# A gated convolution and attention kernel: the loads as streams of their own on SyncE's queue, without GpSimd's fills, the filter's first half early, in a new order

## The chip, the cores and the metric

The kernel runs on one core of one Trainium2 chip. The metric is the device time of one execution in microseconds (us), the median of several runs. The core has five engines with queues of their own: TensorE (PE, matmuls and their weight loads, PEld), VectorE (DVE), ScalarE (ACT), GpSimd (POOL) and SyncE (SP), which here only issues DMAs. Matmuls write to PSUM; DVE and ACT copy ("evict") the results to SBUF.

## The reference

Sequence S = 2048, width D = 640, bfloat16 inputs. Two branches share the input x = A_q, and a gate mixes them.

```
k_shift = sum over t of k_pad[:, t:t+S] * shift_k[:, 3-t]        # four taps along the sequence
kv      = k_shift * v
y       = irfft(rfft(kv, 2S) * rfft(ssm_k, 2S))[:S] + kv * ssm_D # long convolution, per channel
a       = x * y

q, k, v = split(x @ wqkv) in 32 heads of 20
logits  = q . k at offsets 0, 2, ..., 14 back in the sequence, scaled, masked
b       = (softmax(logits) @ v) @ wo

g       = sigmoid(sum(x * gate_w))
out     = g * a + (1 - g) * b
```

## The kernel before

**Attention.** x is loaded in 8 tiles `xn` and transposed by PE into `xT` (`xpose`). `vproj` makes the values `VW` in two halves (weights `Wv0`, `Wv1`, both in `WvT`). `qkproj` makes q and k in five feature groups `ft` of 128 columns: for each `ft`, six units of five matmuls each for q (w = 0) and for k (w = 1). `ft` 0 uses the weights `W0` (spread by `spread` into `Wqk`), the others `W1`, the rest of `Wqk`. Units are evicted into one staging tile `stg` for q and one for k, by DVE (L247) or ACT (L245); GpSimd copies the rows of each head from `stg` into `qb` and `kb` by DMAs (`fragger`, L637: 70 in all). A staging tile is written again only when the copies of the group before it have landed. `score_gen` then makes the scores of eight groups of four heads, t = 0 to 7 (L659), ACT takes their exponentials into `ETall` (L667), `pv_gen` multiplies them with `VW` (L691), and DVE divides into `VW`'s place (L701, L703). Scores of t need the copies of every piece of its heads: t = 1 some of `ft` 1, t = 4 some of `ft` 3, t = 6 some of `ft` 4.

**Convolution.** The four taps run on DVE over `kin`, a part of the tile `KX` (L474 to L489, 56 instructions of 128x1280), then kv = k_shift * v in `vin` (L493). The filter and kv go through a transform in two matmul stages: `s1_unit` (L722 for the filter, L718 for kv) and `s2_unit` with the constants `G` (L741). The filter goes in two halves P = 0 and 1, loaded into the same tile `h_lin`; half 0 is evicted into the tile `H`, half 1 into `SX`, which takes the place of `KX` when the taps are done. kv is evicted into `UC`. Products (L773), a first inverse stage (L852), the attention's output projection (L886) and the last stage with the final sum (`final`, L929 to L946) follow. `Dz` (ssm_D) is added to the filter by one DVE instruction for each half (L790) ahead of its first stage. The gate is one group of matmuls (L541) with one activation on ACT (L545).

**Order.** Every piece of work is a generator that yields requests for engines. A string `ORDER`, one letter for each grant, says which generator goes on next and so sets the order of instructions on every engine; nothing is reordered on the chip, and an engine waits where the next instruction in its queue isn't ready. The costs and landing times in the requests do not reach the chip; they were for the making of the string.

**Loads.** `heads` issues on SyncE, ahead of all: x, `Wv0`, `W0`, then the tap weights `wraw`, the first k rows, `W1` and `Wv1`. All other loads belong to `bulk(ft)`, which `fragger` calls after each feature group: after `ft` 0 the rest of k, its corners, `F`, `wgz`, `Dz` and the filter's first half, after `ft` 1 `G` and half of v, after `ft` 2 the rest of v, after `ft` 3 the filter's second half. Most go through `paced`: GpSimd first writes one element of the destination, and the DMA on SyncE's queue waits for that fill. Each load on SyncE's queue also waits until the eighth before it has landed.

Of the kernel before, what the change touches and what calls it, by code (L numbers as in the profile page):

```python
# [17 lines left out]
S = 2048  # L18
# [109 lines left out]


# [88 lines left out]
def kernel(  # L218
# [105 lines left out]
    st = {}  # L324

    def load(name, dst, src, us, deps=()):
        g = yield Req("S", 600.0, deps, move=us)
        nc.sync.dma_start(dst, src)  # L328
        mark(name, g, 1500.0 if name[0] == "k" else 0.0)
# [6 lines left out]
    def load_k(k):  # L336
        n0, n1 = KROWS[k]
        for q in range(4):
            yield from paced(f"k{k}{q}", kin[32 * q:32 * q + 32, 3 + n0:3 + n1, :], raw(k2, n0 * D + QC * q, [[64 * D, 32], [D, n1 - n0], [1, QC]]), 62.0 * (n1 - n0))

    def load_corners():
        for q in range(4):
            for a, b in ((1, 17), (17, 32)):
                yield from load(f"kh{q}{a}", kin[32 * q + a:32 * q + b, 0:3, :], raw(k2, (64 * a - 3) * D + QC * q, [[64 * D, b - a], [D, 3], [1, QC]]), 90.0)

    def load_h(P):
        if P:
            yield Req("N", 0.0, [ev("hs10")])
        for q in range(4):
            for c in range(2):  # L350
                yield from paced(f"h{P}{q}{c}", h_lin[32 * q:32 * q + 32, :, c, :],
                                 raw(A_ssm_k, (160 * q + 80 * c + PL * P) * S, [[64, 32], [S, PL], [1, 64]]), 1280.0)

    def load_G(a):
        yield from paced(f"G{a}", G[:, 8 * a:8 * a + 8], raw(cf["G"].ap(), 3 * a * 128 * 512, [[512, 128], [128 * 512, 3], [1, 512]]), 1300.0)

    def load_v(c, q):
        yield from paced(f"v{q}{c}", vin[32 * q:32 * q + 32, c], raw(v2, QC * q + 80 * c, [[64 * D, 32], [D, 64], [1, 80]]), 2550.0)

    def small():  # L360
        g = yield Req("G", 1200.0)
        nc.gpsimd.memset(wgz[:], 0.0)
        nc.gpsimd.memset(Dz[:], 0.0)
        yield from load("F", F[:], cf["F"].ap(), 640.0, [g.done])
        yield from load("wgz", wgz[:, :, 0], gate_w.rearrange("(t p) -> p t", p=128), 200.0)
        yield from load("Dz", raw(Dz, 0, [[32 * Dz[:].ap[0][0], 4], [1, 160]]), raw(A_ssm_D, 0, [[160, 4], [1, 160]]), 100.0)

    def bulk(ft):
        if ft == 0:
            yield from load_k(1)  # L370
            yield from load_k(2)
            yield from load_corners()
            yield from small()
            yield from load_h(0)
        if ft == 1:
            for a in range(4):
                yield from load_G(a)
                yield from load_v(0, a)
        if ft == 2:
            for a in range(4):  # L380
                yield from load_v(1, a)
        if ft == 3:
            yield from load_h(1)
# [19 lines left out]
    def heads():  # L403
        z = pab[:, 0].rearrange("p n c -> p (n c)")
        nc.vector.memset(z, 0.0)
        wu = PS[:, 0]
        for n in range(WARM):
            nc.tensor.matmul(wu[:, n % 2, :], lhsT=z[:, 0:128], rhs=z[:, 0:512], start=True, stop=True, skip_group_check=True)
        nc.scalar.dma_start(ident[:], ca["ident"].ap())
        nc.scalar.dma_start(mm[:], ca["mm"].ap())  # L410
        at("ET", 4000.0)
        for a in range(8):
            if a == 1:
                nc.sync.dma_start(Wv[:, :, 0:320], W3[:, :, 2, 0:320])
# [7 lines left out]
        n0, n1 = KROWS[0]  # L422
        for q in range(4):
            nc.sync.dma_start(wraw[32 * q:32 * q + 32].rearrange("p c j -> p (c j)"), raw(A_shift_k, 4 * QC * q, [[0, 32], [1, 4 * QC]]))
        for q in range(4):
            nc.sync.dma_start(kin[32 * q:32 * q + 32, 3 + n0:3 + n1, :], raw(k2, n0 * D + QC * q, [[64 * D, 32], [D, n1 - n0], [1, QC]]))
        for q in range(4):
            at(f"k0{q}", LAND["k"][0])
        for w in range(2):
            nc.sync.dma_start(Wqk[:, :, w, 128:D], W3[:, :, w, 128:D])  # L430
            at(f"W1{w}", LAND["W1"])
        nc.sync.dma_start(Wv[:, :, 320:640], W3[:, :, 2, 320:640])
        at("Wv1", LAND["Wv1"])
# [134 lines left out]
    def qkproj():  # L568
        free = [None] * NSTG
        def unit(ft, w, k):  # L570
# [6 lines left out]
            for i in range(2):  # L577
# [10 lines left out]
                if not ft:  # L588
# [1 line left out]
                    nc.vector.scalar_tensor_tensor((ksets if w else qsets)[0][:, cols].rearrange("p (b k) -> p b k", k=wd), src, own,  # L590
                                                   mm[:, BK * (1 - w):BK * (1 - w) + wd].unsqueeze(1).to_broadcast([128, 3, wd]), ALU.mult, ALU.add)
# [30 lines left out]
    def fragger():  # L622
# [4 lines left out]
        for ft in range(NDT):  # L627
            for w in range(2):
# [359 lines left out]
```

## Time and profile before

| | us |
|---|---|
| runs: median (lowest) of 3 | 225.23 (225.09; one of 483.92) |
| profiled execution: its time | 226.57 |
| profiled execution: span from first to last instruction | 224.6 |
| busy: PE, DVE, ACT, POOL | 206.6, 190.3, 174.8, 49.8 |
| mean granted TensorE clock | 0.972 |

The page gives for each engine the busy time in the span; the views of the trace give single instructions (start, duration, engine, line, output and input tiles), who waited for whom, and busy times in chosen stretches. SPq and POOLq are the instructions with which SyncE and GpSimd issue DMAs; "to landing" is the time from such an issue until the data has arrived.

### The profile page before, as it was taken

To read this page: it belongs to the slowest core of one execution; us is meant where nothing else is said; L and a number is where in the kernel's file an instruction comes from. 1 tells how busy PE (TensorE), PEld (TensorE's weight loads), DVE (VectorE), ACT (ScalarE), POOL (GpSimd) and SP (SyncE) were. 2 spreads that over 40 slices of the span, in tenths; PEclk is the share of its full clock that TensorE was granted. 3 is DMA by queue.
4 is the path that set the end of the run, shared out by engine and by line. 5 is a ranking of instruction groups with operands and counts; after the bars stand their busy time and mean duration, and the time that the engine had idled before them with its cause. 6 is when DMAs were issued, how large, how long until landed. Compare 5 with 4: busy or idle time off the path is not lost.

```text
span 224.6 us, 8413 instructions
## 1 busy us (share of the span) xinstructions
PE 206.6 (92%) x3577; PEld 167.4 (75%) x3577; DVE 190.3 (85%) x277; ACT 174.8 (78%) x253; POOL 49.8 (22%) x132
## 2 busy tenths in 40 slices
PE   7999899999999999999996888999999999988880
PEld 3776677796768658666784767888988999977870
DVE  4787996999988988998888765899999999848991
ACT  2146672559999997899999898999899987767770
POOL 7900673180526047104520000000000000000000
PEclk9999999999999999999999758999999999999997
DMA  7999359889999999976834288777660390001755
GB/s 206 348 238 304 54 97 217 134 150 144 208 172 196 152 163 166 162 107 107 158 85 117 61 175 181 174 203 183 144 191 0 81 236 16 3 3 35 176 140 127
DMA packets 68916, 32.67 MB, mean 145 GB/s; under 512 B 51504, under 2 KB 66736, under 8 KB 68880
## 3 DMA queue, kind: packets, MB, share of 16 engines
q1 hardware_dynamic: 65488, 27.14, 59.5%
q0 software_dynamic: 2944, 4.74, 10.4%
q8 instruction: 28, 0.46, 1.0%
q10 hardware_dynamic: 448, 0.26, 0.5%
q14 instruction: 8, 0.07, 0.1%
HBM read 19.52 MB, written 2.62 MB: 99 GB/s over the span
## 4 chain that ended last, share of the span: by engine, by line
PE 62%; DMA 9%; DVE 8%; ACT 8%; SPq 4%; issue 4%; POOL 2%; ACTq 0%; DVEq 0%; POOLq 0%
PE PS L583 13%; PE PS L886 9%; PE PS L852 8%; PE PS L741 7%; PE PS L691 7%; PE PS L528 6%; DMA xn<-in_A_q_dram 5%; PE PS L659 4%; DMA WvT<-in_B_wqkv_dram 3%; SPq L328 3%; ACT ETall L667 2%; PE PS L722 2%; ACT H L245 2%; PE PS L870 2%; DVE SX L247 2%
## 5 line engine op out<-in xcount | busy, mean ns | idle before, releaser
L667 ACT ACTIVATE ETall<-PS 121x912 bf16<-121x912 f32 (+1 forms) x80 | 64.8, 868 | 7.5 <-PE PS L659 6.7
L583 PE MATMUL PS<-xT,Wqk 128*128 128x342 bf16 (+1 forms) x300 | 50.7, 310 | 0.4 <-ACT xT L245 0.2
L245 ACT CAST UC<-PS 128x1024 bf16<-128x1024 f32 (+2 forms) x48 | 43.9, 1010 | 5.4 <-PE PS L852 3.4
L583 PEld LDWEIGHTS <-Wqk 128*128 128x128 bf16 x300 | 27.9, 97 | 14.0 <-issue 0.6
L528 PE MATMUL PS<-WvT,xT 128*121 128x320 bf16 x180 | 29.6, 302 | 0.6 <-ACT ETall L667 0.5
L637 POOL DMA_DIRECT2D qb<-stg x35 | 17.7, 507 | 52.3 <-ACT stg L245 39.1
L245 ACT CAST stg<-PS 128x363 bf16<-128x363 f32 (+1 forms) x34 | 15.8, 467 | 12.7 <-DVE kb L590 4.6
L474 DVE TENSOR_TENSOR KX<-KX 128x1280 bf16<-128x1280 bf16 x32 | 25.3, 819 | 0.3
L528 PEld LDWEIGHTS <-xT 128*121 128x121 bf16 x180 | 22.8, 134 | 2.6 <-issue 0.4
L886 PE MATMUL PS<-wo,oT 128*128 128x320 bf16 x160 | 24.1, 302 | 0.0
L886 PEld LDWEIGHTS <-oT 128*128 128x128 bf16 x160 | 21.1, 146 | 1.1
L741 PEld LDWEIGHTS <-G 64*128 64x128 bf16 x512 | 19.0, 97 | 3.8 <-issue 1.9
L691 PEld LDWEIGHTS <-ETall 121*128 121x128 bf16 x576 | 18.4, 99 | 2.2 <-issue 0.9
L637 POOL DMA_DIRECT2D kb<-stg x35 | 17.4, 503 | 10.1 <-ACT ETall L667 4.0
L691 PE MATMUL PS<-VW,ETall 121*128 121x63 bf16 (+2 forms) x576 | 19.0, 188 | 0.6 <-ACT ETall L667 0.6
L247 DVE CAST UC<-PS 128x1024 bf16<-128x1024 f32 x14 | 16.7, 1219 | 3.4 <-PE PS L852 3.0
L659 PE MATMUL PS<-qb,kb 31*128 31x114 bf16 x576 | 16.3, 218 | 2.9 <-ACT ETall L667 1.0
L659 PEld LDWEIGHTS <-kb 31*128 31x128 bf16 x576 | 9.6, 96 | 11.6 <-issue 10.5
L852 PE MATMUL PS<-F,Hw 128*128 128x128 bf16 x160 | 18.1, 219 | 0.0
L852 PEld LDWEIGHTS <-Hw 128*128 128x128 bf16 x160 | 17.9, 114 | 0.1
L247 DVE CAST stg<-PS 128x342 bf16<-128x342 f32 (+1 forms) x26 | 13.5, 519 | 2.9 <-PE PS L583 2.0
L703 DVE TENSOR_TENSOR VW<-PS,rd 114x960 bf16<-114x960 f32 (+1 forms) x16 | 14.5, 907 | 0.6
(79 smaller groups left out, 340.3 us busy)
## 6 DMA issues: line engine op xcount, KB each, us to landing
xn<-in_A_q_dram SPq DMA_DIRECT2D x8, 320.0 KB, 6.2
h_lin<-in_A_ssm_k_dram SPq DMA_DIRECT2D x16, 160.0 KB, 4.5
vin<-in_A_v_dram SPq DMA_DIRECT2D x8, 320.0 KB, 11.4
Hw<-H SPq DMA_DIRECT2D x8, 320.0 KB, 3.7
q<-in_A_q_dram SPq DMA_DIRECT2D x8, 320.0 KB, 6.7
Hw<-SX SPq DMA_DIRECT2D x8, 320.0 KB, 4.6
out_dram<-q SPq DMA_DIRECT2D x16, 120.0 KB, 2.2
kb<-stg POOLq DMA_DIRECT2D x22, 85.1 KB, 5.1
```

The source lines that it names most:

```text
L245: nc.scalar.copy(dst, src)
L247: nc.vector.tensor_copy(dst, src)
L474: eng.tensor_tensor(d, kin[:, n + 3 - j:n + 3 - j + m, :], w.to_broadcast([128, m, QC]), ALU.mult)
L528: nc.tensor.matmul(ps[0:BK, 0:320], lhsT=xT[:, dt, s0:s0 + BK], rhs=Wv[:, dt, 320 * hp:320 * hp + 320], start=(dt == 0), stop=(dt == NDT - 1))
L583: nc.tensor.matmul(ps[:, 0:n], lhsT=Wqk[:, dt, w, 128 * ft:128 * ft + 128], rhs=xT[:, dt, s0:s0 + n], start=(dt == 0), stop=(dt == NDT - 1))
L637: nc.gpsimd.dma_start((ksets if w else qsets)[t % 3][r0:r0 + rows, 0:wd], stg[s0:s0 + rows, 0:wd])
L659: nc.tensor.matmul(psum(g, h4 // 2)[:, h4 % 2, BQ * bb:BQ * bb + BQ], lhsT=kb[r:r + DH + NF, BK * b:BK * b + 128], rhs=qb[r:r + DH + NF, B ...
L667: nc.scalar.activation(ETall[0:BK, e, :, 0:BQ * nb], psum(g, k)[0:BK, :, 0:BQ * nb], ACT.Exp, scale=SCALE)
L691: nc.tensor.matmul(O[:, (b - b0) // 6, c0:c0 + 21 * nh], lhsT=ETall[0:BK, e, hh, BQ * bb:BQ * bb + 128], rhs=VW[0:BK, b, 4 * t + h4:4 * t ...
L741: nc.tensor.matmul(ps[:, c, 160 * jj:160 * jj + 160], lhsT=G[rows, j0 + jj, 64 - 64 * rr:192 - 64 * rr], rhs=Am[rows, rr].rearrange("p o ( ...
L852: nc.tensor.matmul(d, lhsT=st[(key, P)][:, c, o + il // 4, :, il % 4], rhs=M[:, k, :], start=(k == 0), stop=(k == 1), skip_group_check=True)
L886: nc.tensor.matmul(op, lhsT=oT[:, ft].rearrange("p h m a -> p a (h m)")[:, t, :], rhs=wo[:, ft, 320 * n:320 * n + 320], start=(ft == 0), s ...
```

## The change

`paced` and its fills on GpSimd are gone, and so is `bulk`. The loads become generators of their own, each granted in `ORDER` by its own letter: `load_W` (W1, Wv1), `load_k` (tap weights, all k rows, corners), `load_h(P)`, `load_G` (F, Dz, G) and `load_v` (wgz, v). Their order on SyncE's queue is that of the new string. The zero fills of `Dz` and `wgz` move to the head of GpSimd's program. DVE's staging cast of `ft` 0 now names the eviction before it (`r.done`) as its dependence.

```
-    def paced(name, dst, src, us):
-        g = yield Req("G", 150.0)
-        nc.gpsimd.memset(dst[:, 0, 0:1], 0.0)
-        yield from load(name, dst, src, us, [g.done])
+    def load_W():
+        for w in range(2):
+            yield from load(f"W1{w}", Wqk[:, :, w, 128:D], W3[:, :, w, 128:D], 2000.0)
+        yield from load("Wv1", Wv[:, :, 320:640], W3[:, :, 2, 320:640], 1250.0)
...
+    def load_k():
         for q in range(4):
+            yield from load(f"wr{q}", wraw[32 * q:32 * q + 32].rearrange("p c j -> p (c j)"), ...
+        for k, (n0, n1) in enumerate(KROWS):
+            for q in range(4):
+                yield from load(f"k{k}{q}", kin[32 * q:32 * q + 32, 3 + n0:3 + n1, :], ...
...
     def load_h(P):
         if P:
             yield Req("N", 0.0, [ev("hs10")])
         for q in range(4):
             for c in range(2):
-                yield from paced(f"h{P}{q}{c}", h_lin[32 * q:32 * q + 32, :, c, :],
+                yield from load(f"h{P}{q}{c}", h_lin[32 * q:32 * q + 32, :, c, :],
...
-    def bulk(ft):
-        if ft == 0:
-            yield from load_k(1)
-            yield from load_k(2)
-            yield from load_corners()
-            yield from small()
-            yield from load_h(0)
-        if ft == 1:
-            for a in range(4):
-                yield from load_G(a)
-                yield from load_v(0, a)
...
-            yield from bulk(ft)
...
-                r = yield Req("AD", n=m, deps=[g.done] + ([free[sb]] if free[sb] is not None else []), give=g.banks)
+                r = yield Req("AD", n=m, deps=[r.done if not ft else g.done] + ([free[sb]] if free[sb] is not None else []), give=g.banks)
...
 ORDER = """
-a-aa-aw6-ww-wa-awa6-aiaiiw-6-6aiai-i-aa-aiiaiiiiii-iiiaiiiiidiwidi-wiiiiififiiwfcwcidcwficcicwccdfddfccfccfcfwicxd-iwwfcxxfdic-xcc
+a-aa3-a-333a-yy-a3a33zav-yaiii3-yi-aiz3uavi-3zaiaz-a3ii3aii3i3iii33i3-3vaiii3i-i-3iiiiiii33iv-ivcdcidi3ciccc-3iid3d3zfdwi3czzwid-3
...
```

SyncE's queue behind the x tiles (`xn`), before: tap weights (in_A_shift_k), first k rows, the W1 halves (`Wqk`), Wv1 (`WvT`), and then the loads that wait for fills.

```order
L424 DMA KX<-in_A_shift_k_dram 32x640 x4
L426 DMA KX<-in_A_k_dram 32x22x160 x4
L430 DMA Wqk<-in_B_wqkv_dram 128x5x512 x2
L432 DMA WvT<-in_B_wqkv_dram 128x5x320
L328 DMA KX<-in_A_k_dram 32x22x160 x4
L328 DMA KX<-in_A_k_dram 32x20x160 x4
```

The same place now, up to Wv1; nothing here waits for a fill.

```order
L328 DMA h_lin<-in_A_ssm_k_dram 32x40x64 x2
L328 DMA KX<-in_A_shift_k_dram 32x640 x2
L328 DMA KX<-in_A_k_dram 32x22x160
L328 DMA h_lin<-in_A_ssm_k_dram 32x40x64
L328 DMA F<-cf_F 128x512
L328 DMA h_lin<-in_A_ssm_k_dram 32x40x64 x2
L328 DMA Dz<-in_A_ssm_D_dram 4x160
L328 DMA h_lin<-in_A_ssm_k_dram 32x40x64
L328 DMA KX<-in_A_k_dram 32x22x160 x3
L328 DMA Wqk<-in_B_wqkv_dram 128x5x512
L328 DMA KX<-in_A_k_dram 32x22x160
L328 DMA WvT<-in_B_wqkv_dram 128x5x320
```

The eight loads of the filter's first half, which before stood behind all of k, now stand ahead of most of k, of the second half of W1 and of Wv1 (two filter loads, the first W1 half and two tap weights stand above these rows). The second half of the filter stands between the loads of v and G, and waits for the first half's last matmul (L693 now, L722 before).

DVE where `ft` 1's first q unit is staged (`stg`, 128x342), before; the taps (TENSOR_TENSOR on `KX`) have begun ahead of it.

```order
L497 COPY KX<-KX 128x640
L474 TENSOR_TENSOR KX<-KX 128x1280
L590 SCALAR_TENSOR_TENSOR kb_80<-PS,mm 128x363
L474 TENSOR_TENSOR KX<-KX 128x1280 x2
L590 SCALAR_TENSOR_TENSOR kb_80<-PS,mm 128x363
L483 TENSOR_TENSOR KX<-KX 128x1280
L474 TENSOR_TENSOR KX<-KX 128x1280
L487 TENSOR_TENSOR KX<-KX 128x1280
L489 TENSOR_TENSOR KX<-KX 128x1280
L474 TENSOR_TENSOR KX<-KX 128x1280
L247 CAST stg<-PS 128x342
```

The same place now.

```order
L562 SCALAR_TENSOR_TENSOR kb_80<-PS,mm 128x363
L469 COPY KX<-KX 128x640
L247 CAST VW<-PS 121x16x20
L247 CAST stg<-PS 128x342
L247 CAST VW<-PS 121x16x20
L761 TENSOR_TENSOR h_lin<-h_lin,Dz 128x80
L247 CAST stg<-PS 128x342 x2
L247 CAST VW<-PS 121x16x20
L247 CAST stg<-PS 128x342
L446 TENSOR_TENSOR KX<-KX 128x1280 x3
```

The taps have moved behind the four staging casts, and the sum of Dz to the filter's first half stands between them.

ACT ahead of the exponentials of t = 4 (`ETall`, the last row), before. The k units of `ft` 3 (`stg`, 128x363) were staged further up, the last five of them by DVE.

```order
L667 ACTIVATE ETall<-PS 121x2x342 x2
L245 CAST VW<-PS 121x16x20 x2
L245 CAST H_302<-PS 128x2x512 x2
L245 CAST stg<-PS 128x342
L245 CAST VW<-PS 121x16x20
L245 CAST stg<-PS 128x342
L245 CAST H_302<-PS 128x2x512
L245 CAST VW<-PS 121x16x20
L245 CAST H_302<-PS 128x2x512
L667 ACTIVATE ETall<-PS 121x2x456 x6
```

The same place now.

```order
L245 CAST stg<-PS 128x363
L638 ACTIVATE ETall<-PS 121x2x342
L245 CAST stg<-PS 128x363
L245 CAST VW<-PS 121x16x20
L638 ACTIVATE ETall<-PS 121x2x342
L245 CAST VW<-PS 121x16x20
L245 CAST H_336<-PS 128x80x12 x2
L638 ACTIVATE ETall<-PS 121x2x456 x2
```

The k units of `ft` 3 are now staged just ahead of t = 4; the evictions of `H` here are those of the second stage (128x80x12) and no longer those of the first (128x2x512). Behind the gate's activation and ahead of the first eviction of `UC`, ACT had 34 exponentials, 7 evictions of `H`, 10 of `SX` and 4 staging casts; it now has 24, 2, 9 and none.

More of the change, by code (lines that the diff above doesn't have):

```diff
@@ L326, in load @@
     def load(name, dst, src, us, deps=()):
-        g = yield Req("S", 600.0, deps, move=us)
+        g = yield Req("S", 450.0, deps, move=us)
         nc.sync.dma_start(dst, src)
-        mark(name, g, 1500.0 if name[0] == "k" else 0.0)
-    def paced(name, dst, src, us):
-        g = yield Req("G", 150.0)
-        nc.gpsimd.memset(dst[:, 0, 0:1], 0.0)
-        yield from load(name, dst, src, us, [g.done])
-    def load_k(k):
-        n0, n1 = KROWS[k]
+        mark(name, g)
+    def load_W():
[3 more added lines that the diff above has]
+    def load_k():
         for q in range(4):
-            yield from paced(f"k{k}{q}", kin[32 * q:32 * q + 32, 3 + n0:3 + n1, :], raw(k2, n0 * D + QC * q, [[64 * D, 32], [D, n1 - n0], [1, QC]]), 62.0 * (n1 - n0))
-    def load_corners():
+            yield from load(f"wr{q}", wraw[32 * q:32 * q + 32].rearrange("p c j -> p (c j)"), raw(A_shift_k, 4 * QC * q, [[0, 32], [1, 4 * QC]]), 200.0)
+        for k, (n0, n1) in enumerate(KROWS):
+            for q in range(4):
+                yield from load(f"k{k}{q}", kin[32 * q:32 * q + 32, 3 + n0:3 + n1, :], raw(k2, n0 * D + QC * q, [[64 * D, 32], [D, n1 - n0], [1, QC]]), 62.0 * (n1 - n0))
         for q in range(4):
             for a, b in ((1, 17), (17, 32)):
-                yield from load(f"kh{q}{a}", kin[32 * q + a:32 * q + b, 0:3, :], raw(k2, (64 * a - 3) * D + QC * q, [[64 * D, b - a], [D, 3], [1, QC]]), 90.0)
+                yield from load(f"kh{q}{a}", kin[32 * q + a:32 * q + b, 0:3, :], raw(k2, (64 * a - 3) * D + QC * q, [[64 * D, b - a], [D, 3], [1, QC]]), 150.0)
     def load_h(P):
@@ L350, in load_h @@
             for c in range(2):
-                yield from paced(f"h{P}{q}{c}", h_lin[32 * q:32 * q + 32, :, c, :],
[L352 to L365, printed above, removed]
-        yield from load("Dz", raw(Dz, 0, [[32 * Dz[:].ap[0][0], 4], [1, 160]]), raw(A_ssm_D, 0, [[160, 4], [1, 160]]), 100.0)
-    def bulk(ft):
-        if ft == 0:
-            yield from load_k(1)
-            yield from load_k(2)
-            yield from load_corners()
-            yield from small()
-            yield from load_h(0)
-        if ft == 1:
-            for a in range(4):
-                yield from load_G(a)
-                yield from load_v(0, a)
[L379 to L383, printed above, removed]
+                yield from load(f"h{P}{q}{c}", h_lin[32 * q:32 * q + 32, :, c, :],
+                                raw(A_ssm_k, (160 * q + 80 * c + PL * P) * S, [[64, 32], [S, PL], [1, 64]]), 1050.0)
@@ new lines, in load_G, with load_v @@
+    def load_G():
+        yield from load("F", F[:], cf["F"].ap(), 640.0)
+        yield from load("Dz", raw(Dz, 0, [[32 * Dz[:].ap[0][0], 4], [1, 160]]), raw(A_ssm_D, 0, [[160, 4], [1, 160]]), 100.0)
+        for a in range(4):
+            yield from load(f"G{a}", G[:, 8 * a:8 * a + 8], raw(cf["G"].ap(), 3 * a * 128 * 512, [[512, 128], [128 * 512, 3], [1, 512]]), 1500.0,
+                            [ev("Wp00"), ev("Wp01")])
+    def load_v():
+        yield from load("wgz", wgz[:, :, 0], gate_w.rearrange("(t p) -> p t", p=128), 500.0)
+        for c in range(2):
+            for q in range(4):
+                yield from load(f"v{q}{c}", vin[32 * q:32 * q + 32, c], raw(v2, QC * q + 80 * c, [[64 * D, 32], [D, 64], [1, 80]]), 2800.0)
@@ L421, in heads @@
             at(f"x{a}", LAND["x"][a])
[L422 to L433, printed above, removed]
+        nc.gpsimd.memset(Dz[:], 0.0)
+        nc.gpsimd.memset(wgz[:], 0.0)
         nc.gpsimd.memset(xT[:, :, 0:X0], 0.0)
@@ L495, in conv @@
     def conv():
-        yield Req("D", 570.0, [ev("k00")])
+        yield Req("D", 570.0, [ev("k00")] + [ev(f"wr{q}") for q in range(4)])
         nc.vector.tensor_copy(wl, wraw.rearrange("p c j -> p j c"))
@@ L535, in gate @@
     def gate():
-        g = yield Req("P", 0.0, [ev("vproj0"), ev("vproj1")] + xdeps(0, HS), take=1, pe=(20, 50.0, 110.0, 53.0))
+        g = yield Req("P", 0.0, [ev("vproj0"), ev("vproj1"), ev("wgz")] + xdeps(0, HS), take=1, pe=(20, 50.0, 110.0, 53.0))
         gps = psum(g)[:, 0]
@@ L787, in h_slot @@
         for P in range(2):
-            g = yield Req("D", 150.0, [ev(f"h{P}{q}{c}") for q in range(4) for c in range(2)])
+            g = yield Req("D", 150.0, [ev(f"h{P}{q}{c}") for q in range(4) for c in range(2)] + [ev("Dz")])
             h_ = h_lin[:, :, :, 0]
@@ L802, in h_stream @@
     def h_stream(P):
-        yield Req("N", 0.0, [ev(f"Dz{P}"), ev("SX" if P else "H0")])
+        yield Req("N", 0.0, [ev(f"Dz{P}"), ev("F"), ev("SX" if P else "H0")])
         yield from transform("h", P)
@@ L950 @@
     for gen in (xpose, h0_slot, fragger, score_gen, pv_gen, conv, conv_v, conv_end, qkproj, gate, x_slot, h_slot, p2_slot,
-                u_slot, swaps, load_T, load_wo, op_tr, outproj, final):
+                u_slot, swaps, load_T, load_wo, op_tr, outproj, final, load_W, load_k, load_G, load_v, spread):
         plan.add(gen(), gen.__name__)
-    for gen in (load_q, vproj, h_stream, u_stream, products, inverse1):
+    for gen in (load_h, load_q, vproj, h_stream, u_stream, products, inverse1):
         for P in range(2):
             plan.add(gen(P), f"{gen.__name__}{P}")
-    plan.add(spread(), "spread")
     plan.run(ORDER)
```

16 lines of the change are left out of this document (8 added, 8 removed).

## The prediction

> **What bounds the kernel now.** I read the page's first part, then the busy times by stage, then the waits and the groups inside the one stage that stands out.
>
> ```profile
> span 224.6 us, 8413 instructions
> PE 206.6 (92%) x3577; PEld 167.4 (75%) x3577; DVE 190.3 (85%) x277; ACT 174.8 (78%) x253; POOL 49.8 (22%) x132
> ```
>
> TensorE (PE) is busy for 92% of the span, and VectorE (DVE) and ScalarE (ACT) are not far below. An average of 92% can hide a stage with another limit, so the stages come next. I cut them at the first attention product, the gate, the end of the projections, the first matmul of the value transform (L718) and the last tiles. The columns are length, then busy time and count of PE, weight loads, DVE, ACT and POOL, then granted clock, DMA share and GB/s.
>
> ```profile
> 0.00:48.30 48.30, 45.23 (x393) 33.81 (x394) 38.93 (x64) 23.28 (x43) 24.25 (x61) 1.00 0.87 194
> 48.30:98.75 50.45, 50.26 (x853) 36.55 (x854) 45.98 (x70) 44.86 (x70) 17.30 (x52) 1.00 1.08 170
> 98.75:109.70 10.95, 10.79 (x212) 7.04 (x213) 9.94 (x14) 10.65 (x17) 3.50 (x7) 1.00 0.64 114
> 109.70:143.56 33.86, 28.20 (x701) 23.62 (x700) 25.56 (x32) 31.22 (x40) 4.03 (x10) 0.85 0.58 126
> 143.56:155.00 11.44, 11.16 (x107) 10.06 (x106) 11.11 (x11) 11.44 (x14) 0.19 (x1) 1.00 0.89 222
> 155.00:199.40 44.40, 44.37 (x738) 41.88 (x735) 40.95 (x69) 38.71 (x51) 0.54 (x2) 1.00 0.38 89
> 199.40:219.50 20.10, 16.61 (x587) 14.48 (x587) 16.99 (x22) 14.64 (x22) 0.00 (x0) 1.00 0.40 99
> ```
>
> Three things are to be seen. Up to 109.7 us PE hardly stops after the first loads, while ACT is busy only 23.28 of the first 48.30 us. From 109.70 to 143.56 us PE loses 5.66 us and its clock falls to 0.85, while ACT is busy 92%: this stage belongs to ACT. From 155 to 199.4 us PE is the limit again. The change fills ACT's idle front with the filter's first half; its gain, if any, must show in the fourth row.
>
> **The loads.** SyncE's queue before, and the price of GpSimd's staging copies with quiet and with loaded DMA engines:
>
> ```profile
> 16.89 1.06 SPq L432 DMA_DIRECT2D WvT<-in_B_wqkv_dram  x1
> 30.68 14.10 SPq L328 DMA_DIRECT2D KX<-in_A_k_dram  x16
> 47.00 9.87 SPq L328 DMA_DIRECT2D h_lin<-in_A_ssm_k_dram  x8
> 24.14 3.12 POOL L637 DMA_DIRECT2D qb<-stg  x6 [12.37 <-ACT stg L245]
> 20.00:30.00 10.00, 8.92 (x85) 6.64 (x86) 8.73 (x15) 7.08 (x15) 5.56 (x11) 1.00 0.51 127
> qb<-stg POOLq DMA_DIRECT2D x2, 32.1 KB, 2.9
> qb<-stg POOLq DMA_DIRECT2D x5, 80.2 KB, 6.3
> kb<-stg POOLq DMA_DIRECT2D x1, 68.1 KB, 5.3
> 6.64 6.90 DMA xn<-in_A_q_dram
> ```
>
> The queue lies idle from 17.95 to 30.68 us, because the fills stand behind twelve copies on GpSimd; DMA runs at half share there. The fills themselves (0.1 us each, on an engine busy 22%) are worth nothing on the path. Without them the queue goes on at once. Will the weights be late, now that the filter stands ahead of them? The last x tile lands at 13.5 us (6.64 + 6.90). Ahead of the second half of Wqk stand eight filter loads (9.87 us by the row above), four k loads (4/16 of 14.10 is 3.5 us), the first Wqk and small ones (some 3 us): landing near 32 us with its own transfer. PE reaches the first matmul that reads it only after 39.6 us of its own work in the new order (summed at the prices of the next part), so nothing waits, with about 8 us of cover; if the cover were gone, DVE's convolution would also stand behind the k loads, microsecond for microsecond.
>
> **ACT's backlog behind the gate.** The work that PE has moved to in front of the gate's matmuls is, by the two orders, 35 projection matmuls, 72 scores, 72 attention products and 96 second-stage filter matmuls. Their prices:
>
> ```profile
> 71.00 0.72 PE PS L583 x5
> 51.92 0.32 PE PS L659 x16
> 109.69 1.45 PE PS L691 x48
> 142.27 1.36 PE PS L741 x36
> 99.99 0.60 ACT L545 ACTIVATE WvT<-PS 128x512 f32<-128x512 f32 x1 [0.22 <-PE PS L541]
> 145.30 1.01 ACT L245 CAST UC<-PS 128x1024 bf16<-128x1024 f32 x1
> ```
>
> That is 7 x 0.72 + 4.5 x 0.32 + 1.5 x 1.45 + 2.67 x 1.36 = 12.3 us, so ACT's gate activation, which ended at 100.59, ends near 112.9. What ACT then still has to do before the first eviction of the value transform, priced from these groups:
>
> ```profile
> L667 ACT ACTIVATE ETall<-PS 121x912 bf16<-121x912 f32 x48 | 42.5, 947 | 1.9 <-PE PS L659 1.7
> L667 ACT ACTIVATE ETall<-PS 121x684 bf16<-121x684 f32 x32 | 22.2, 750 | 5.6 <-PE PS L659 5.0 <-PE PS L691 0.5
> L245 ACT CAST H<-PS 128x960 bf16<-128x960 f32 x6 | 5.3, 1004 | 0.0
> L245 ACT CAST SX<-PS 128x1024 bf16<-128x1024 f32 x4 | 3.9, 1036 | 0.0
> L245 ACT CAST SX<-PS 128x960 bf16<-128x960 f32 x5 | 4.5, 971 | 0.7 <-PE PS L741 0.7
> L245 ACT CAST SX<-PS 128x640 bf16<-128x640 f32 x1 | 0.7, 694 | 0.0
> L245 ACT CAST stg<-PS 128x363 bf16<-128x363 f32 x19 | 8.9, 469 | 6.3 <-DVE kb L590 4.6 <-PE PS L583 1.6
> ```
>
> Before: 18 exponentials of 947, 16 of 750, six H evictions of 1004, four SX of 1036, five of 971, two short ones of 0.69 and four staging casts of 0.47 are 47.3 us; they took 145.30 - 100.59 = 44.7 us, 0.945 of the sum, since neighbours overlap. After: 12 x 0.947 + 12 x 0.750 + 1.0 + 3 x 1.036 + 5 x 0.971 + 2 x 0.69 = 30.7 us, by the same ratio 29.0. So the value transform begins at 112.9 + 29.0 = 141.9 instead of 145.3 us: 3.4 us sooner, or 2.6 if PE needs 5 to 6% more than such bare sums in front of the gate, as between 48.30 and 98.75 us (50.45 us for sums of 48.0). I take **-3.0**. The ends: 0, if ACT reaches the gate late; -11, if ACT and DVE hide and PE alone (20 us of matmuls behind the gate) set the stage.
>
> **The staging copies stand closer.** Two staging tiles serve five groups of heads, so the first q eviction of the second group waits until all six q copies of the first have landed. By PE's new order 5.6 us of matmuls lie between (15 projections, 20 of the value projection at the same 0.14 us each, 32 scores). What is needed is an eviction (0.5), six issues (3.1) and one landing: 2.9 us with quiet engines, 6.3 with loaded ones, 6.5 to 9.9 us in all. Before, these copies fell into the idle 20 to 30 us; now the queue is full there. The waiting cast is at the head of DVE, and behind it stand a value eviction, the filter's Dz sum for which PE's first filter matmuls wait, three more staging casts and the first taps. The wait is 0.9 to 4.3 us on DVE; PE has four PSUM slots of work in hand, so I take **+2.0** between 0 and +4.3.
>
> The same holds before the scores of head groups 1, 4 and 6 (t = 1, 4, 6). PE work between the last staged projection and these scores shrinks from 7.3, 8.9 and 7.4 us to 4.7, 3.5 and 4.5. Eviction, issue and landing (0.5 + 0.5 + 5.3 with loaded engines for t = 4) need 6.3 us: 2.8 too much; t = 6 by the same sum about 0.9, t = 1 from 0 to 2.5. While PE waits there, ACT and DVE work off what is queued, so I count half of 2.8 + 0.9: **+1.8**, between 0 and +6.2.
>
> **The convolution starts later.** Its first taps move from 23.5 us to about 39 us, behind the k loads; some 9 us of DVE work go into the stretch up to the gate, where DVE is at 45.98 of 50.45 us. It gives back about as much, since fewer evictions fall to it. I take 0, up to +4 if DVE becomes the bound there. The tail (143.56 us on) keeps its matmuls; oT copies and a few evictions change between DVE and ACT: 0, give or take 1.
>
> Sum against the profiled execution (226.57 us, its span 224.6): -3.0 + 2.0 + 1.8 = +0.8, so 227.4. The median of the runs shown is 225.23, 1.3 below that execution; the same +0.8 gives **226.0 us**, no change that can be told.
>
> **The rivals.** *Faster, by the clock.* The slow stage in slices of 5 us:
>
> ```profile
> 115.00:120.00 5.00, 4.11 (x116) 3.39 (x111) 4.54 (x5) 5.00 (x7) 0.00 (x0) 1.00 0.07 25
> 130.00:135.00 5.00, 4.63 (x96) 3.57 (x96) 3.12 (x7) 4.47 (x6) 0.19 (x1) 0.51 0.87 192
> PE PS L722 <- ACT ETall L667: 1.2, 3, 0.6
> ```
>
> PE runs at half clock at 130 to 135 us, although none of its waits in this stage is longer than 0.6 us for ACT. If the filter's first half, gone from here, lets PE keep its clock, the stage gives back up to 0.15 x 28.2 = 4.2 us more: 225.23 - 3.0 - 4.2 = 218.0. Against it: the new order leaves 20 us of matmuls in 29 us of ACT work, 69% as against 71% now (28.2 x 0.85 in 33.86), so the clock should drop again. The Trainium skill, in "TensorE: Matmul & The Clock Gate", section "Part 1: The HAM clock gate (the "warmup" mystery)", halves the clock after an idle window of about 3.4 us; by that rule the stage would lose nothing today, and the trace contradicts it. Its section "A second HAM failure mode: psum-queue depth-cycling" lets short idles between groups of matmuls make the gate oscillate, and with that the trace agrees (0.51 with waits of 0.6 us).
>
> *Slower, by the loaded engines.* The fills had kept SyncE's loads away from the copies. If every copy lands as with loaded engines and each wait goes through in full, the sum is -3.0 + 4.3 + 6.2 = +7.5, or 232.7 us; it decides from the point where a landing of over 5 us meets the 3.5 us ahead of t = 4. For it: 6.3 against 2.9 us. Against it: before, landings of that size were hidden.
>
> *The loads aren't earlier after all.* SyncE's queue is in order, and the second half of the filter (it needs the first half's matmuls done) stands ahead of most of v and half of G. Then the front stays as it is: 225.2 us.
>
> **How the numbers follow.** The forecast (222 to 230 us) has 0.57, the clock 0.20, loaded engines 0.20, no effect 0.03. The range that leaves out about 2 in 10 cuts into both rivals: 219.5 to 231.5. A measurement here can tell 2% (4.5 us) from no change. Faster by more than that (under 220.7) takes the clock's 0.20, slower (over 229.7) the loaded engines' 0.20 and 0.02 of the forecast's edge: 0.20, 0.58, 0.22.
>
> **What would show it.** Right: DVE waits for DMA qb<-stg at 32 to 38 us; PE waits for kb<-stg ahead of t = 4; the first UC eviction near 142 to 146 us; a granted clock below 0.9 there again. Wrong: PE without any wait from 30 to 110 us and UC before 138 us (the first rival), or PE waiting for Wqk, WvT or k in the front.

## The result, and the profile after

The changed kernel takes 241.5 us (median of 4 runs, 240.26 to 242.91); the kernel before took 225.16 us beside it. The ratio is 1.073 (95% interval 1.065 to 1.081): **slower by 16 us**, well above the forecast of 226.0 and above its range. The profiled execution took 240.95 us, its span 239.2. Three of the traces further down (the old order with the new order of loads, the first form with all loads short, and the run with only v and the filter's second half short) are of slow executions, 0.8 to 2.3% above the median of their runs, so single times in them are a little long.

The page after, then the stretches up to the first attention product, the gate, the first matmul of the value transform (L689 now), and the end. The last row here cuts the new kernel once more, at that matmul alone, and the two rows of the next block cut the kernel before at the same place. Columns as in the prediction.

```profile
span 239.2 us, 8354 instructions
PE 211.7 (89%) x3577; PEld 170.1 (71%) x3577; DVE 189.0 (79%) x271; ACT 178.9 (75%) x259; POOL 47.5 (20%) x96
...
0.00:47.80 47.80, 39.83 (x359) 28.93 (x360) 25.41 (x45) 21.34 (x36) 16.87 (x32) 0.93 1.04 206
47.80:126.80 79.00, 72.04 (x1163) 52.30 (x1165) 68.84 (x98) 63.74 (x103) 25.47 (x51) 0.98 0.72 122
126.80:159.08 32.28, 28.21 (x646) 22.74 (x645) 25.16 (x31) 28.38 (x38) 4.03 (x10) 0.74 0.52 133
159.08:239.20 80.12, 71.67 (x1420) 66.12 (x1418) 69.63 (x101) 65.45 (x85) 1.10 (x3) 0.99 0.48 111
...
0.00:159.08 159.08, 140.08 (x2160) 103.97 (x2160) 119.41 (x171) 113.45 (x175) 46.37 (x93) 0.91 0.78 149
```

```profile
0.00:143.56 143.56, 134.48 (x2152) 101.01 (x2152) 120.41 (x177) 110.02 (x168) 49.08 (x129) 0.96 0.86 163
143.56:224.60 81.04, 72.13 (x1428) 66.42 (x1426) 69.87 (x101) 64.79 (x86) 0.72 (x3) 0.99 0.47 114
```

The whole loss lies ahead of the value transform, which starts 15.5 us later (159.08 against 143.56); behind it the new kernel is 0.9 us shorter. Of the 15.5 us, 9.9 are time in which PE stands still (159.08 - 140.08 = 19.0 against 143.56 - 134.48 = 9.1) and 5.6 are the same matmuls at a lower clock (140.1 against 134.5 us busy).

Where PE stands still, in slices of 5 us, and the instructions at the first stop (start, duration, engine, line, in brackets the idle time before and its releaser), from the same trace:

```profile
30.00:35.00 5.00, 3.88 (x42) 2.71 (x41) 0.49 (x1) 3.45 (x5) 1.27 (x3) 1.00 1.18 226
35.00:40.00 5.00, 0.36 (x10) 0.22 (x9) 1.32 (x4) 0.00 (x0) 2.00 (x4) 0.91 1.27 177
40.00:45.00 5.00, 5.00 (x28) 2.76 (x24) 2.23 (x6) 2.28 (x3) 0.00 (x0) 0.50 1.06 122
...
27.04 3.22 POOL L609 DMA_DIRECT2D qb<-stg  x6 [15.32 <-ACT VW L245]
35.33 0.50 POOL L609 DMA_DIRECT2D kb<-stg  x1 [3.08 <-DMA qb<-stg]
38.67 0.52 DVE L247 CAST stg<-PS 128x342 bf16<-128x342 f32 x1 [7.62 <-DMA qb<-stg]
39.64 0.47 PE L630 MATMUL PS<-qb,kb 31*128 31x114 bf16 x10 [5.76 <-DVE VW L247]
40.79 4.46 PE L555 MATMUL PS<-xT,Wqk 128*128 128x342 bf16 x15
```

GpSimd issues the six q copies of `ft` 0 from 27.04 to 30.26 us. The DMA engines are full, and DVE's first staging cast of `ft` 1 gets its turn only at 38.67, 8.4 us after the last issue. PE, behind DVE, does nothing for 5.76 us. When it goes on, its clock is 0.50 for 5 us, and 15 projection matmuls take 4.46 us (2.34 us at full clock in a run below).

How long those copies took to land, by the issues between 26 and 34 us (KB each, median us):

```profile
KX<-in_A_k_dram SPq DMA_DIRECT2D x4, 220.0 KB, 11.6
qb<-stg POOLq DMA_DIRECT2D x2, 32.1 KB, 9.0
kb<-stg POOLq DMA_DIRECT2D x1, 51.0 KB, 8.3
```

9.0 us (the other four q copies 8.5 to 9.0), where the same copies landed in 2.9 us before (the others 2.3 to 2.9). Apart from one wait of 0.5 us for x, every wait of PE, DVE and ACT for a DMA that this trace lists is for such a copy; none is for k, v, the filter or the weights. The stop repeats where later groups need a staging tile back, and in front of scores. These are the longest waits of PE (waited for, us in total, times, longest), one piece of the chain of waits, two staging casts of later groups on ACT, the slices at 80, 85 and 105 us, and three slices behind the gate:

```profile
PE PS L630 <- DVE VW L247: 5.8, 1, 5.8
PE PS L555 <- ACT stg L245: 3.1, 1, 3.1
PE PS L630 <- DMA kb<-stg: 2.6, 3, 2.0
PE PS L555 <- ACT VW L245: 1.5, 1, 1.5
...
49.80 8.35 DMA qb<-stg
...
59.20 0.44 ACT L245 CAST stg<-PS 128x342 bf16<-128x342 f32 x1 [2.09 <-DMA kb<-stg]
82.07 0.44 ACT L245 CAST stg<-PS 128x342 bf16<-128x342 f32 x1 [3.72 <-DMA qb<-stg]
...
80.00:85.00 5.00, 2.43 (x46) 1.86 (x46) 2.13 (x4) 2.53 (x5) 2.60 (x6) 0.85 1.18 175
85.00:90.00 5.00, 5.00 (x68) 3.46 (x67) 4.47 (x7) 3.71 (x7) 0.00 (x0) 0.81 0.98 168
105.00:110.00 5.00, 3.02 (x79) 2.45 (x74) 4.86 (x7) 2.90 (x5) 2.67 (x6) 1.00 0.66 138
135.00:140.00 5.00, 4.56 (x84) 3.87 (x83) 3.31 (x5) 4.44 (x6) 0.00 (x0) 0.50 0.56 167
140.00:145.00 5.00, 4.54 (x91) 3.69 (x88) 3.88 (x4) 4.32 (x7) 0.00 (x0) 0.50 0.55 130
145.00:150.00 5.00, 4.61 (x101) 3.73 (x102) 3.76 (x5) 3.56 (x5) 0.19 (x1) 0.50 0.49 115
```

### The profile page after: what moved, and what is told of

The parts are those of the page before. It is cut to its first block, busy times and chain, and to the rows that moved or that the text cites. A ratio compares the mean times of both kernels' runs of the same rounds, so it can differ in the third digit from the quotient of the medians.

```text
span 239.2 us, 8354 instructions
## 1 busy us (share of the span) xinstructions
PE 211.7 (89%) x3577; PEld 170.1 (71%) x3577; DVE 189.0 (79%) x271; ACT 178.9 (75%) x259; POOL 47.5 (20%) x96
## 4 chain that ended last, share of the span: by engine, by line
PE 49%; DMA 17%; issue 9%; SPq 8%; ACT 7%; DVE 5%; POOL 3%; DVEq 0%; POOLq 0%; ACTq 0%
PE PS L555 10%; PE PS L857 8%; SPq L328 7%; PE PS L712 7%; PE PS L823 6%; DMA qb<-stg 6%; PE PS L662 5%; DMA KX<-in_A_k_dram 5%; ACT UC L245 4%; DMA kb<-stg 4%; PE PS L630 3%; PE PS L500 3%; DMA G<-in_B_wqkv_dram 2%; POOL qb L609 2%; PE PS L841 2%
## 5 line engine op out<-in xcount | busy, mean ns | idle before, releaser
L555 PE MATMUL PS<-xT,Wqk 128*128 128x342 bf16 (+1 forms) x300 | 54.2, 324 | 4.5 <-ACT stg L245 3.1
L245 ACT CAST UC<-PS 128x1024 bf16<-128x1024 f32 (+2 forms) x45 | 41.8, 1021 | 4.7 <-PE PS L823 4.1
L245 ACT CAST stg<-PS 128x363 bf16<-128x363 f32 (+1 forms) x42 | 19.3, 472 | 19.4 <-DMA qb<-stg 3.7
L500 PE MATMUL PS<-WvT,xT 128*121 128x320 bf16 x180 | 30.8, 304 | 0.1
L630 PE MATMUL PS<-qb,kb 31*128 31x114 bf16 x576 | 17.2, 227 | 10.6 <-DVE VW L247 5.8
L857 PE MATMUL PS<-wo,oT 128*128 128x320 bf16 x160 | 25.1, 303 | 0.0
L247 DVE CAST stg<-PS 128x342 bf16<-128x342 f32 (+1 forms) x18 | 9.5, 527 | 15.5 <-DMA qb<-stg 7.6
L247 DVE CAST UC<-PS 128x1024 bf16<-128x1024 f32 (+2 forms) x17 | 19.7, 1188 | 1.4 <-issue 0.8
L662 PE MATMUL PS<-VW,ETall 121*128 121x63 bf16 (+2 forms) x576 | 19.9, 191 | 0.0
L245 ACT CAST VW<-PS 121x320 bf16<-121x320 f32 x24 | 10.4, 438 | 8.3 <-PE PS L500 8.0
```

Source lines behind the costliest of these rows:

```text
L245: nc.scalar.copy(dst, src)
L247: nc.vector.tensor_copy(dst, src)
L500: nc.tensor.matmul(ps[0:BK, 0:320], lhsT=xT[:, dt, s0:s0 + BK], rhs=Wv[:, dt, 320 * hp:320 * hp + 320], start=(dt == 0), stop=(dt == NDT - 1))
L555: nc.tensor.matmul(ps[:, 0:n], lhsT=Wqk[:, dt, w, 128 * ft:128 * ft + 128], rhs=xT[:, dt, s0:s0 + n], start=(dt == 0), stop=(dt == NDT - 1))
L630: nc.tensor.matmul(psum(g, h4 // 2)[:, h4 % 2, BQ * bb:BQ * bb + BQ], lhsT=kb[r:r + DH + NF, BK * b:BK * b + 128], rhs=qb[r:r + DH + NF, B ...
L662: nc.tensor.matmul(O[:, (b - b0) // 6, c0:c0 + 21 * nh], lhsT=ETall[0:BK, e, hh, BQ * bb:BQ * bb + 128], rhs=VW[0:BK, b, 4 * t + h4:4 * t ...
```

## The experiments

Two theories. **A, crowding:** SyncE's loads now run beside GpSimd's copies; the copies land late, and the shorter distances of the new order turn that into stops. **B, the order:** the new compute order is too tight even with quiet DMA engines. Each ratio is against runs of the kernel before on the same chip, with its 95% interval.

**The old order without the fills.** The loads and the compute order stay; only `paced` loses its fill, and the zero fills of `Dz` and `wgz` move to the head of GpSimd's program.

```
     def paced(name, dst, src, us):
-        g = yield Req("G", 150.0)
-        nc.gpsimd.memset(dst[:, 0, 0:1], 0.0)
-        yield from load(name, dst, src, us, [g.done])
+        yield from load(name, dst, src, us)
```

> The old order and the old loads, without GpSimd's fills: SyncE's queue no longer waits behind the copies, nothing else moves. Theory A (loads that run beside the staging copies make them land late, and the distance decides whether PE feels it): the copies of ft 0 land in 5 to 8 us instead of 2.9, DVE's first cast of ft 1 waits some us, most of it covered by the old distances: 226 to 232 us. Theory B (the new order is at fault by itself, the fills are worth nothing): 224 to 226 us. If the fills alone carried the old kernel's time: 238 us or more.

226.56 us, ratio 1.005 (1.001 to 1.009). The copies' landing (issues of 22 to 30 us) and DVE's longest wait for them:

```profile
qb<-stg POOLq DMA_DIRECT2D x2, 32.1 KB, 5.8
...
DVE stg L247 <- DMA qb<-stg: 2.1, 1, 2.1
```

The copies take twice as long (5.8 against 2.9 us), and the old distances hide nearly all of it. The fills alone are worth about 1 us.

**The old order with the new order of loads.** SyncE's queue up to Wv1 as in the changed kernel, no fills, the compute order of before. In the string, z stands for the filter's first half, w for the tap weights, k and l for the first and second k rows, u for W1 and Wv1.

```
-        for q in range(4):
-            nc.sync.dma_start(wraw[32 * q:32 * q + 32]...
...
+        for c in "zwzuwzzwwkzFzzDzkkkulu":
+            early(c, n.get(c, 0))
...
```

> The old compute order behind the new order of loads up to Wv1 (filter's first half ahead of k and of the second half of Wqk), no fills. If late copies cost only where the distances are short: the old distances cover most of it, 226 to 230 us, with a wait for Wqk or WvT at most. If the new order of loads costs by itself, whatever runs behind it: 234 us or more.

238.3 us, ratio 1.051 (1.040 to 1.061): the second answer, but only in part by the copies:

```profile
PE PS L670 <- ACT stg L245: 9.9, 1, 9.9
PE PS L670 <- DMA kb<-stg: 3.3, 1, 3.3
...
DVE KX L485 <- DMA KX<-in_A_k_dram: 9.8, 1, 9.8
```

In the old order the taps stand early on DVE and wait 9.8 us for the first k rows, now behind the filter, and PE waits for 9.9 us behind them. A late copy costs PE another 3.3 us. So the early filter can't be had with the old order as it stands; the later taps of the new one avoid the wait for k. What the old distances would cost beside the new loads without that wait, this run can't tell.

**The new order with short loads.** Theory B needs quiet engines to be seen. k's later rows are cut to one row a load, v and the filter's second half to two; GpSimd zeroes `KX` and `vin` once.

```
-... kin[32 * q:32 * q + 32, 3 + n0:3 + n1, :], ...
+... kin[32 * q:32 * q + 32, 3 + n0:3 + n0 + (1 if k else n1 - n0), :], ...
...
+        nc.gpsimd.memset(KX[:, 0:45 * QC].bitcast(F32), 0.0)
```

> The new order with nearly empty transfers: k's second and third part shortened to one row a load, v and the filter's second half to two, GpSimd zeroes these tiles in its idle first 25 us; weights, first k rows, the filter's first half and G as before. It leaves out most of k, v and half of the filter. Theory A (crowded DMA engines): copies land in 3 to 4 us, the stops of PE at 55 to 62, 80 to 85 and 105 to 110 us go, that at 35 to 40 at least halves; t = 6 stays: 222 to 230 us. Theory B (the distances of the new order are too short even with quiet engines): 236 to 242 us.

229.37 us, ratio 1.019 (1.012 to 1.026): 12 of the 16 us come back. The slices at 35, 55, 80 and 105 us:

```profile
35.00:40.00 5.00, 2.46 (x23) 1.41 (x23) 1.68 (x4) 2.03 (x3) 1.50 (x3) 0.66 0.73 178
55.00:60.00 5.00, 4.97 (x72) 3.57 (x71) 4.56 (x7) 4.32 (x8) 1.76 (x4) 1.00 0.38 96
80.00:85.00 5.00, 5.00 (x107) 4.06 (x96) 4.93 (x9) 4.43 (x8) 1.16 (x3) 1.00 0.06 10
105.00:110.00 5.00, 5.00 (x124) 3.92 (x124) 4.61 (x7) 4.42 (x9) 0.29 (x1) 1.00 0.01 3
```

All stops but the first are gone. That one is shorter (PE waits 3.4 us instead of 5.8), though the copies were expected in 3 to 4 us and took 6.8. There the filter's first half, the first k rows and the weights still run beside the copies.

**All loads short**, in two forms. The first cuts the first k rows and the filter's first half too:

```
-... h_lin[32 * q:32 * q + 32, :, c, :], ...
+... h_lin[32 * q:32 * q + 32, 0:2, c, :], ...
```

> As the run with short loads, and the first k rows and the filter's first half also shortened (one row and two rows a load; GpSimd zeroes the tiles); weights and G stay whole. It leaves out nearly all of k, v and the filter. If the stop at 35 to 40 us, which the short loads left (DVE waits 5.3 us there), is made by these 2.2 MB in front of and beside the copies: the wait falls under 2 us, 221 to 225 us. If it is the order's own (5.6 us of matmuls against six issues and a landing): the wait stays over 3 us, 227 to 230 us.

229.09 us, ratio 1.015 (1.005 to 1.025), and DVE still waits 5.4 us. This doesn't tell the theories apart: SyncE's queue waited for the zeroing of `h_lin` until 18.65 us, which put the second half of Wqk (issued at 28.67) and Wv1 (30.79) beside the copies. The second form puts the weights ahead:

```
 SyncE behind x:  h0, tap weights,
+                 W1, W1, Wv1,
                  h0, tap weights, h0, ... k ...
-                 W1 (between h0 and tap weights), W1 and Wv1 (among k)
```

> As the run with all loads short, with the second part of the weights ahead of the short loads, so that nothing large runs beside the copies of ft 0 (there the zeroing had pushed 1 MB of weights beside them, and DVE still waited 5.4 us). It leaves out nearly all of k, v and the filter. If crowding explains the stop at 35 to 40 us: the copies land in about 3 us, the wait falls under 2 us, PE keeps its clock, the gate's matmuls come near 111 us and the time is 222 to 226 us, no better than the old kernel. If the new order itself makes the stop: the wait stays over 3 us, 227 to 230 us.

227.6 us, ratio 1.009 (1.005 to 1.012). The time is that foretold for the order's own fault, but the stop at 35 to 40 us is gone. PE waits 3.13 us for a cast of DVE instead, until 18.09: a copy of DVE from SBUF to SBUF and the three instructions behind it, begun between 13.5 and 14.9 us, all end at 18.0, as GpSimd's zeroing of `KX` does (13.41 to 17.97). The zeroing of `h_lin`, moved ahead of GpSimd's other head work, had pushed it there. The last form lessens that: the filter's first half whole, the zeroing behind the other head work, the weights first.

> As the run with short loads (filter's first half, weights and G whole), with the first k rows short too and the second part of the weights ahead of the filter; the zeroing is behind GpSimd's other head work again, since in the run before it cost PE 3 us at 14 to 18 us. It leaves out nearly all of k, v and half of the filter. Crowding as the only cause: no stop at 35 to 40 us, gate's matmuls at 110 to 113 us, 222 to 225.5 us, the old kernel's time or a little less. If the order costs something with quiet engines too: 227 us or more.

**224.97 us, ratio 0.997 (0.994 to 1.001).** Slices at 35 and 40 us, the copies' landing, and what follows the gate:

```profile
35.00:40.00 5.00, 4.89 (x49) 3.25 (x47) 3.80 (x9) 3.32 (x6) 0.98 (x2) 1.00 0.84 204
40.00:45.00 5.00, 5.00 (x103) 3.86 (x102) 4.97 (x7) 3.48 (x5) 3.48 (x7) 1.00 0.43 89
...
qb<-stg POOLq DMA_DIRECT2D x2, 32.1 KB, 2.8
...
L515 PE MATMUL PS<-xT,wgz x20: 379/379/389, 111.9 to 112.8; 128*32 128x512 bf16 x20
113.20 0.61 ACT L519 ACTIVATE WvT<-PS 128x512 f32<-128x512 f32 x1
112.80:145.40 32.60, 26.44 (x642) 21.62 (x635) 25.32 (x31) 28.36 (x39) 4.05 (x10) 0.84 0.52 134
L245 ACT CAST UC<-PS x45: 703/1023/1131, 145.4 to 199.8; 128x1024 bf16<-128x1024 f32 x26, 128x960 bf16<-128x960 f32 x18, 128x640 bf16<-128x640 f32 x1
```

With copies that land in 2.8 us the new order runs without the stop and is as fast as the old kernel, within 0.6%. Theory B falls as an account of the loss: without the crowding none of it is left. The new order's gain is hardly there either: the first UC eviction comes at 145.4 us, against 145.30 before. But a part of it is hidden, since the zeroing still makes PE wait for DVE at 16.52 us:

```profile
PE PS L557 <- DVE VW L247: 1.6, 1, 1.6
```

Without this wait the run would be some 1.6 us shorter, by an estimate from this row. And the old order was not run with short loads, so what quiet engines alone are worth to the old kernel isn't known.

**Which loads crowd.** One fill back, so that k from the sixth load on waits for all copies of `ft` 0:

```
             for q in range(4):
+                if (k, q) == (1, 1):
+                    g = yield Req("G", 150.0)
+                    nc.gpsimd.memset(kin[32:64, 3 + n0, 0:1], 0.0)
                 yield from load(f"k{k}{q}", ...
```

> The new order with one fill put back: the k loads from the sixth on wait on SyncE's queue until GpSimd has issued all twelve copies of ft 0. If the k loads behind the weights are what delays the copies of ft 0: DVE's wait falls from 7.6 to under 3 us, PE keeps its clock at 40 to 45 us: 232 to 236 us. If it is what stands ahead of them (second half of Wqk, Wv1, the filter): the wait stays above 6 us, 239 to 243 us.

> As the run with one fill, and the second part of the weights (both halves of Wqk and Wv1) ahead of the filter on SyncE's queue, as in the old kernel. If the weights' 1 MB beside the copies of ft 0 is what delays them: DVE's wait falls under 3 us and the time to 230 to 235 us, 3 us or more below the run with the fill alone. If the crowding by any loads counts, the filter takes the weights' place and it is within 2 us of that run.

240.4 us (1.066; 1.058 to 1.073) with the fill, 238.58 (1.061; 1.051 to 1.071) with the weights ahead of the filter as well. DVE's wait at this place is 6.0 and 5.6 us, against 7.6, and the q copies land in 7.5 and 6.1 us, against 9.0. The two times can't be told apart, as their intervals overlap. Neither the later k loads nor the weights are the culprit alone: in the first run the weights still run beside the copies (issued up to 28.75 us), in the second the filter and the first k rows have moved into their place.

Only the loads of the later stops short, v and, in the same way, the filter's second half:

```
-... vin[32 * q:32 * q + 32, c], ...
+... vin[32 * q:32 * q + 32, c, 0:2], ...
```

> The new kernel with only v and the filter's second half short (two rows a load), k and all else whole. It leaves out most of v and of half the filter. If each stop has its own crowding: those at 80 to 85 and 105 us go with their slow clock, 4 to 6 us, 235 to 238 us, while those at 35 to 40 and 55 to 62 stay. If the late stops only follow from the early ones: 239.5 us or more.

234.01 us, ratio 1.036 (1.029 to 1.043), a little more than expected of it. Slices at 35, 80 and 105 us:

```profile
35.00:40.00 5.00, 0.32 (x4) 0.10 (x3) 0.62 (x2) 0.00 (x0) 2.01 (x4) 1.00 1.14 148
80.00:85.00 5.00, 5.00 (x91) 3.70 (x89) 4.62 (x8) 4.40 (x8) 3.94 (x8) 1.00 0.32 72
105.00:110.00 5.00, 4.84 (x73) 3.44 (x65) 4.93 (x8) 4.95 (x8) 0.71 (x2) 1.00 0.28 76
```

The first stop stays, the late ones go: each has its own crowd, and the late ones, with the slow clock behind them, cost about 7.5 us.

**The staging tile.** Is it the wait for a free tile that passes the late copies on? Here `ft` 0 is staged in `vin`, which is empty then, so that `ft` 1 finds both staging tiles free:

```
-stgs[w] = pL.tile([128, KW], BF, name="stg", tag=f"stg{sb}"), []
+stgs[w] = (pL.tile([128, KW], BF, name="stg", tag=f"stg{sb}") if ft else
+           vin[:].rearrange("p c n i -> p (c n i)")[:, KW * w:KW * w + KW]), []
```

> The new kernel, with the two staging tiles of ft 0 in the tile vin, which is free then; ft 1 no longer waits for the copies of ft 0, and nothing else moves. If DVE's wait for these copies is the whole of the stop at 35 to 40 us (PE waits of 5.8 and 3.1, and half clock for 5 us behind it): the stop goes and 6 to 9 us with it, 232 to 236 us; the stops at 55 to 62, 80 to 85, 105 and 130 us stay. If the crowded copies hold up the next user instead (the scores of t = 1): 239 to 243 us.

> As the run with ft 0 staged in vin, and the second part of the weights ahead of the filter on SyncE's queue. If the weights are late behind the filter once the cast no longer waits: 2 us or more faster than that run, 229 to 234 us. If not: within 1.5 us of it.

> The old kernel with ft 0 staged in vin. Its PE loses only about 1 us at 25 to 30 us, and its longest wait there isn't for a copy: 224 to 226 us, no change. If staging had limited the old order too: 221 us or less.

236.15 us (1.051; 1.045 to 1.057), 235.44 (1.049; 1.041 to 1.057) with the weights first, and 224.94 (0.999; 0.996 to 1.003) for the old kernel staged so. In the first of them:

```profile
35.00:40.00 5.00, 5.00 (x84) 3.87 (x82) 4.53 (x7) 4.13 (x8) 2.95 (x6) 1.00 1.19 154
50.00:55.00 5.00, 0.12 (x1) 0.10 (x1) 0.88 (x2) 0.95 (x3) 1.00 (x2) 0.72 1.17 187
...
43.93 9.48 DMA qb<-stg
47.44 2.34 PE L556 MATMUL PS<-xT,Wqk 128*128 128x342 bf16 x15
54.12 0.51 DVE L247 CAST stg<-PS 128x342 bf16<-128x342 f32 x1 [5.28 <-DMA kb<-stg]
```

The stop at 35 to 40 us is gone although the DMA engines are as full as before, and 5.3 us with it (6 to 9 were expected). One group later, where the tiles run out again, a copy takes 9.48 us and PE stops from 50 to 55 us instead. So the staging tile is the link at the first stop, and one more pair only moves the stop. At the second stop there is another link: GpSimd itself waits until earlier copies have landed before it issues the next (3.45 us ahead of 35.99 and 2.38 us ahead of 43.42), so the copies of `ft` 1 are issued late as well as landing late. The weights make no difference here that can be told (0.7 us), and no wait of PE in either trace names them: they weren't late. The old kernel gains nothing, since its copies were hidden.

No run beat the kernel before.

## Why the prediction was wrong

**The mechanism was named, its size was not.** The order of places was right: DVE waits for qb<-stg up to 38.67 us (foretold: 32 to 38), then PE waits for kb<-stg at t = 1, 4 and 6. What came is the rival of the loaded engines, which had 0.20 and 232.7 us; that sum, too, was 9 us short.

**The staging term (+2.0, between 0 and +4.3) is the step that failed**, in three ways. PE's waits behind staging casts (5.8, 3.1 and 1.5 us) come to 10.4 us, and slower matmuls follow them.

- *The landing.* Its upper end took 6.3 us from copies of the old kernel's loaded stretches. Here the copies took 9.0. The row came from a queue that the fills had held back; without them it was no bound. With 9.0 in the term's own sum the wait is 0.5 + 3.1 + 9.0 - 5.6 = 7.0 us, and DVE waited 7.62: the form of the sum held, and the landing in it was mis-sized. The old order without fills showed 5.8, so what the new order puts beside them adds as much again.
- *Counted once.* I priced the wait between the first and the second group. Two staging tiles serve five groups, and the new distances are short for all: the casts at 59.20 and 82.07 us wait for copies in the same way, and the run with short v and short second half of the filter gives back 7.5 us, at the late places.
- *The clock.* I let PE work off what it had in hand and counted no slower matmuls. A stop of 5.76 us left the clock at 0.50 for the next 5 us; in all, 5.6 us of the loss are slower matmuls. An estimate from the clocks of the slices puts about 4 us of them behind the stops of 5.8 and 3.1 us (0.50 and 0.90 in the slices at 40 and 45 us, 0.85 and 0.81 at 80 and 85). What is left must lie mostly behind the gate, where the clock was 0.50 from 135 to 150 us without a long stop, and isn't this term's. The Trainium skill, in "TensorE: Matmul & The Clock Gate", section "HAM oscillation — how this bites in real kernels", lets waits of more than about 3.4 us bring on the slow clock. The stop of 5.76 us agrees with that; the one of 3.06 us, after which the clock fell as well, is shorter than the page has it.

**The waits before scores (+1.8, up to +6.2)** came where they were foretold and cost PE 2.6 us in three waits: 0.4 at t = 1, 2.0 at t = 4 and 0.2 at t = 6. This term holds, though its working has a slip: by the sum as written t = 6 comes to 6.3 - 4.5 = 1.8 us, not 0.9.

**ACT's backlog (-3.0) was worth at most half of that in the quiet run**, the only one that can tell. There the gate's activation ends at 113.8 us (foretold 112.9), or some 1.6 us earlier without the zeroing's wait, but from there to the first UC eviction it takes 31.6 us where I had 29.0. So the value transform starts 0.1 us later than before, or, by that estimate, 1.5 us sooner instead of 3.4. I carried over the ratio 0.945 between ACT's time and the sum of its work from this stage of the old kernel, where ACT was busy 94%:

```profile
100.59:145.30 44.71, 38.89 (x888) 31.12 (x885) 35.40 (x43) 41.99 (x55) 7.53 (x17) 0.89 0.61 129
```

With less of the filter behind the gate, ACT is busy only 28.36 of 32.60 us there, 87%: it waits for PE, whose clock is 0.84 and which waits for it and for a copy in turn. ACT's work was about what I had (28.36 us busy, 29.0 foretold with its gaps), but it no longer set the stage's length alone.

**Loads, conv, tail.** SyncE's queue did go on at once, and PE waited for neither Wqk nor WvT, as foretold. The later taps cost nothing that the quiet run shows (it leaves out most of k, though). The tail is 0.9 us shorter, within its 0 +- 1. The other rival, a better clock, is refuted: 0.74 between gate and value transform, and 0.84 in the quiet run.

**The front was full.** Between 20 and 30 us the old kernel's DMA share was 0.51; I took this as room for the filter, and saw that the copies fell into it, but priced its loss by a landing of 6.3 us at most. It was the room in which the copies landed in 2.9 us. The milder crowding of the old order without fills (copies in 5.8 us) costs 1 us, the short distances with quiet engines nothing, the short distances with the full crowding (9.0 us) 16. The old distances with the full crowding were not measured by themselves.

## What to carry to other kernels

A DMA queue that lies idle beside another queue's small, urgent transfers may be what makes them fast: before it is filled, ask who waits for those transfers and with how much work in hand. A landing time is a property of the load on the engines, so a row from a paced stretch is no upper bound for an unpaced one, and a wait that comes from a ring of buffers must be priced for each turn of the ring, with the slow clock behind a long stop. Where a stage is shortened by taking work from its bounding engine, check whether that engine still bounds it before its busy time is turned into a gain.

## What the runs showed of the hardware

- A 32 KB copy within SBUF, issued by GpSimd, landed in 2.8 to 2.9 us with quiet engines, in 5.8 beside k's loads and in 9.0 beside k, the filter and the weights. The share of the DMA engines was over 1 in the last two. The Trainium skill, in "DMA: Bandwidth & Descriptors", section "Queues, rings and completion order", lets each engine take turns between its queues, a packet at a time. That the copies get through at all while SyncE's queue is full agrees with it; where the time of a late copy goes, no run here shows.
- GpSimd itself was held up in this kernel: the ninth copy was issued only at 35.33 us, after 3.08 us of waiting for an earlier copy to land. Late copies delay the issue of the next ones.
- PE's clock was 0.50 in the slice after the 5.76 us stop and fell after one of 3.06 us too (0.85 and 0.81 in those slices). It was 0.74 on the mean between gate and value transform, where no wait of PE was longer than 0.7 us. What brings the clock down there stays open.
- While GpSimd zeroed a large tile (13.41 to 17.97 us, second form with all loads short), a DVE copy from SBUF to SBUF and the three instructions behind it, which take 0.2 to 0.8 us in the changed kernel, ended only when it did, 3.2 to 4.5 us after their start.
